# Two seams of a fused forward and backward kernel: the first load of hh's rows issued by GpSimd, backward's tiles cleared in parts by VectorE, dO's tail rows requested earlier

## Chip, cores and metric

The kernel runs on one core of a Trainium2 chip. The metric is the device time of one execution in microseconds; the time before is the median of three runs. Beside the runs there is one execution under the hardware profiler, and every view of the profile that is shown comes from it. TensorE (PE in the views) multiplies matrices, PEld is its loading of weights, VectorE is DVE, ScalarE is ACT, GpSimd is POOL and SyncE is SP. SyncE, ScalarE and GpSimd also issue transfers, each on a queue of its own.

## The reference

The program returns the output of a transformer block and the gradients of its weights and inputs, in bf16 (S = 2048 tokens, D = 512, F = 1792, 32 heads of 128, segments of 32 tokens with 8 memory rows).

```python
mod = (silu(c) @ w_mod).reshape(1, 6, 1, -1)
sa, ca, ga, sb, cb, gb = (mod[:, i] for i in range(6))
h = layernorm(x) * (1 + ca) + sa
x = x + ga * A(h, mem0, Wq, Wk, Wv, Wo)      # attention, segment by segment
h = layernorm(x) * (1 + cb) + sb
x = x + gb * B(h, w_gate, w_up, w_down)

def A(x, mem0, ...):                         # mem goes from segment to segment
    for s in range(S // 32):
        h = concatenate([mem, x[32 * s:32 * s + 32]])
        q, k, v = h @ Wq, h @ Wk, h @ Wv
        o = softmax(mask(q @ k.T * scale)) @ v @ Wo
        mem, out[s] = o[:8], o[8:]

def B(x, w_gate, w_up, w_down):
    hh = sigmoid(x @ w_gate) * (x @ w_up)
    return hh @ w_down

out, vjp = jax.vjp(block, x, mem0, Wq, Wk, Wv, Wo, w_gate, w_up, w_down, c, w_mod)
return out, *vjp(grad_out)
```

## The kernel before, in words

The program is one long stream with several phases. Two places of it matter here.

The first is the end of phase 3, the GLU forward and backward. It is a pipeline over 16 tiles of 128 tokens with seven stages s0 to s6, deepest stage first in each step (`run_pipeline`), so that step `it` runs stage k on tile it - k. Stage s2 makes the rows of hh (tile `hh`), which GpSimd stores to HHROWS in DRAM (L1087); s3 turns hh into `hhT` by a transposing DMA of SyncE (L1098) and makes du and dg (stored by GpSimd to DUROWS and DGROWS); s4 multiplies hhT by w_down (L1120) and turns du and dg into `duT` and `dgT` (L1123, L1124); s5 multiplies those by the turned weights (L1145) and makes dx, which has a single buffer and is stored to DX1ROWS (L1173); s6 sums rows (L1188), turns da (L1192) and stores it as DAOT (L1196, SyncE).

As the pipeline drains, the gradient of w_down begins, 14 chunks of 128 features, each a chain of 16 products over the 16 token tiles (`wd_chunk`, L1216). Its operands are all the rows of hh, loaded back in groups of 384 features (`load_hr`, L1212, 1536 KB in rows of 768 B for group 0), and the rows of db (`dbr`, loaded by ScalarE at L1228). Both lie where w_gate and w_up were (`Wk`). NT is 16: the hook `after(it)` requests dbr after step 17, group 0 after step 18 and group 1 after step 19, and runs a chunk after each of steps 19, 20 and 21. Groups 0 and 1 are SyncE's, the others ScalarE's. The remaining chunks run in the next stage, between transposes of the attention weights (L1380 and L1367, loaded through `stage`, L1376 and L1362), followed by the gradients of w_gate and w_up (L1301).

The second place is the start of phase 4, the backward of attention, 64 turns from the last segment to the first, with the order of every engine's instructions in the loop written by hand (`pin`). Before the loop the tiles are made: dS, dOst, dKT, dQT, Qst and Kst are cleared whole by GpSimd (`ptiles`, L1430), dOT by VectorE (L1435). Each tile has 11 groups of 128 columns (GW), of which 120 are used in most. Then the first rows of dy are projected into `RBds` (L255), turned into `btd` (`turn_b`, L264), spread into dOT (`to_heads`, L65, GpSimd) and copied as tail rows into `dOst` by three small transfers of GpSimd (`dO_tails`, L1546). A last transfer writes zeros from dS to DHA (L1549). A turn's first copies of RAd into dOst are GpSimd's too (L1660); the turn then begins on TensorE with dVT's products (`gv0`, L1616, named g_ps), which read dOst and Pst, then `dp` (L1593), which reads dOT and VT, and so on to dh_ps (L215). `prod` (L1578) on VectorE needs dOT complete. `get_loads` loads OT, Pst and VT of a turn on SyncE (L1514, L1517), `load_rows` Qst and Kst (L1531).

Outside the hand-written orders a scheduler of the tile framework sets each engine's order; in every engine's queue an instruction that waits holds up those behind it.

Of the kernel before, what the change touches and what calls it, by code (L numbers as in the profile page):

```python
# [40 lines left out]
class K:  # L41
# [915 lines left out]
    def phase3(self):  # L957
        nc, tc, cfg, io = self.nc, self.tc, self.cfg, self.io
        D, DC, F, FC, NT, T = cfg.D, cfg.DC, cfg.F, cfg.FC, cfg.NT, cfg.T
# [7 lines left out]
        with ExitStack() as ctx:  # L967
# [8 lines left out]
            i0 = len(self.traced())  # L976
# [7 lines left out]
            def mm():  # L984
                return psM.tile([128, 512], F32, name="mm", tag="m")
# [218 lines left out]
            hrs = {0: hr_0}  # L1204
# [4 lines left out]

            def load_hr(g):  # L1210
                w = min(384, F - 384 * g)
                (nc.sync if g < 2 else nc.scalar).dma_start(hrs[g][:, :, 0:w], self.HHROWS[:, 384 * g:384 * g + w].rearrange("(j p) f -> p j f", p=128))  # L1212

            def wd_chunk(fc, ps, ot):
                for j in range(NT):
                    nc.tensor.matmul(ps[:], lhsT=hrs[fc // 3][:, j, (fc % 3) * 128:(fc % 3) * 128 + 128], rhs=dbr[:, j, :],  # L1216
                                     start=(j == 0), stop=(j == NT - 1))
                self.evac("act" if kk[0] % 2 == 0 else "dve", ot[:], ps[:])
                kk[0] += 1
                nc.gpsimd.dma_start(io["out_9"][fc * 128:(fc + 1) * 128, :], ot[:])  # L1220

            def after(it):
                for f in turns.pop(it, []):
                    f()
                if it == 2:
                    self.pin(i0, [ET.PE, ET.Activation])
                if it == NT + 1:
                    nc.scalar.dma_start(dbr, self.DBROWS[:, :].rearrange("(j p) d -> p j d", p=128))  # L1228
                elif it == NT + 2:
                    load_hr(0)  # L1230
                elif NT + 3 <= it < NT + 6:
                    if it == NT + 3:
                        load_hr(1)
                    wd_chunk(it - NT - 3, mm(), sbp.tile([128, D], BF16, name="ot2", tag="db", bufs=2))
# [5 lines left out]
            def after(it):  # L1240
# [3 lines left out]
                if it >= 5:  # L1244
                    later(it)

            self.run_pipeline(NT, [s0, s1, s2, s3, s4, s5, s6], deepest_first=True, after=after)
            self.pin(i0, [ET.DVE])
            self.pin_behind(i0, self.pinned, [ET.PE, ET.DVE, ET.Activation, ET.Pool, ET.SP])
# [8 lines left out]
        with ExitStack() as ctx:  # L1258
# [6 lines left out]
            def emit_setup():  # L1265
                done[0] += 1
                while setup_pieces and (n_setup - len(setup_pieces)) * n_chunks < done[0] * n_setup:
                    setup_pieces.pop(0)()
            h2r = self.flat(self.Wk, NT * D, NT * D).rearrange("p (j d) -> p j d", j=NT)
            load_hr(2)  # L1270
            xrs = []

# [125 lines left out]
    def phase4(self):  # L1398
        nc, tc, cfg, io = self.nc, self.tc, self.cfg, self.io
        D, DC, H, E, L, M, T, G, NS = cfg.D, cfg.DC, cfg.H, cfg.E, cfg.L, cfg.M, cfg.T, cfg.G, cfg.NS  # L1400
        GW = 128
# [4 lines left out]
        with self.p4_ctx as ctx:  # L1406
# [18 lines left out]
            def ptiles(name, n, zero=True):  # L1425
                ts = []
                for i in range(n):
                    t = pt.tile([128, G * GW], BF16, name=f"{name}{i}")
                    if zero:
                        nc.gpsimd.memset(t[:], 0.0)  # L1430
                    ts.append(t)
                return ts
# [3 lines left out]
            RAd = pt.tile([128, 8 * 128], BF16, name="RAd")  # L1436
            RBds = [pt.tile([128, 8 * 128], BF16, name=f"RBd{i}") for i in range(2)]
            btd = pt.tile([128, 8, 128], BF16, name="btd")
            dSs = ptiles("dS", 1)
            dSTs = ptiles("dST", 1, zero=False)  # L1440
            dOst_t = ptiles("dOst", 1)[0]
            dXTs = {nm: ptiles(nm, n, zero=nm != "dVT") for nm, n in (("dVT", 1), ("dKT", 1), ("dQT", 1))}

            def part3(t, pi):
                return t[:, pi * PW:min((pi + 1) * PW, G * GW)].rearrange("p (g x) -> p g x", x=GW)
# [17 lines left out]
            def to_heads(eng, src, i0, n, r0, w, o):  # L1463

                b = 0 if w == 32 else 96
                s4 = src.rearrange("p i (j r) -> p i j r", r=32)
                d = dOT[:, 120 * i0:120 * (i0 + n)].rearrange("p (i x) -> p i x", x=120)[:, :, b:b + 3 * w]
                self.evac(eng, d.rearrange("p i (j r) -> p i j r", r=w), s4[:, :, 0:3, o:o + w])
                for g in range(3):
                    lo, hi = max(3 * g, i0), min(3 * g + 3, i0 + n, 8)  # L1470
                    if lo < hi:
                        d = dOT[:, 960 + 120 * g + b + w * (lo - 3 * g):960 + 120 * g + b + w * (hi - 3 * g)]
                        self.evac(eng, d.rearrange("p (i r) -> p i r", r=w), s4[:, lo - i0:hi - i0, 3, o:o + w])
# [9 lines left out]
            def proj_b(t, hf, parts=1):  # L1483
                ps = psb.tile([128, 512], F32, name="pass_ps", tag="dh")

                def part(k):
                    self.col_pass(psp, WoT, hf, lambda c: dbs[t][:, c, :, :].rearrange("p s q -> p (s q)"), None, None, ps,
                                  range(k * DC // parts, (k + 1) * DC // parts))

                part(0)  # L1490

                def rest():
                    for k in range(1, parts):
                        part(k)
                    return lambda: self.evac(("act", "dve")[hf], RBds[t % 2][:, 512 * hf:512 * hf + 512], ps[:])

                return rest

            def turn_b(t):
                tps = [self.turn_half(psp, RBds[t % 2], hf) for hf in range(2)]  # L1500

                def f():
                    for hf in range(2):
                        self.evac(("act", "dve")[hf], btd[:, 4 * hf:4 * hf + 4, :], tps[hf][:])
                return f
# [31 lines left out]
            get_loads(NS - 1)  # L1537
            for hf in range(2):
                proj_b(NS // 4 - 1, hf)()()
            turn_b(NS // 4 - 1)()  # L1540
            to_heads("pool", btd[:], 0, 8, 32, 8, 24)

            def dO_tails(s):
                for j in range(3):
                    o = 32 * j + 8 * (s % 4)
                    nc.gpsimd.dma_start(dOst_t[96 + 8 * j:104 + 8 * j, 0:1024], RBds[(s // 4) % 2][o:o + 8, :])  # L1546

            dO_tails(NS - 1)
            nc.gpsimd.dma_start(self.DHA[NS, 0:M, :], dSs[0][0:M, 0:D])  # L1549
            nseg_t = 128 // T  # L1550
            row_stores = []

# [6 lines left out]
            i0 = len(self.traced())  # L1559
            for s in reversed(range(NS)):  # L1560
# [12 lines left out]
                dS, dST, dOst = dSs[0], dSTs[0], dOst_t  # L1573
                dVT, dKT, dQT = dXTs["dVT"][0], dXTs["dKT"][0], dXTs["dQT"][0]
# [160 lines left out]
                g = s // 4  # L1735
# [428 lines left out]
```

## Time and profile before

| what | value |
|---|---|
| runs, median (lowest to highest) | 3083.14 us (3083.08 to 3084.64) |
| profiled execution, its own time | 3080.64 us |
| its span, first to last instruction | 3078.9 us |
| mean granted TensorE clock | 0.991 |
| busy: TensorE, VectorE, GpSimd, ScalarE | 97%, 52%, 45%, 41% of the span |
| DMA | 703.54 MB, mean 229 GB/s |
| end of the GLU pipeline, start of w_down's gradient | about 1300 to 1345 us from the span's start |
| start of the backward turns | about 1524 to 1550 us |
| one later backward turn | 14.90 us (pass_ps at 1549.77 and 1564.67) |

A line of a view gives the engine, the line of the kernel, the operation, and `out<-in` by the names of tiles. In a list in order of time the first two numbers are start and duration in us; what stands in brackets is the idle time before it and what ended that. SPq, ACTq and POOLq are the engines' queues in which transfers are issued; a transfer's duration there is that of its issue, and its data land later. The list of waits has the waiting line, what released it, the total, the number of times and the longest. The windows give for each stretch the busy time of every engine with the number of instructions, the granted clock (1.00 is full speed), the busy share of the DMA engines, which can pass 1 in a short window, and GB/s.

### The profile page before, as it was taken

Reading aid. Unit: us, or ns where it says so; the run is one execution under the profiler, and the core shown is the slowest. Engines: PE = TensorE matmul, PEld = TensorE weight load, DVE = VectorE, ACT = ScalarE, POOL = GpSimd, SP = SyncE. Lnnn points to the kernel's source line nnn. Section 1 sums busy time; section 2 is a strip of 40 time slices with the busy share of each in tenths; the row PEclk is TensorE's granted clock in tenths of the full one; section 3 lists DMA queues with packets and bytes.
Section 4 is the critical chain, followed back from the end, with each engine's and each line's share of the span. In section 5 each row is a group of like instructions: output and inputs, shape, how many; then the busy total and the mean of one; then the engine's idle time right before and its main releaser. Section 6 shows DMA issues by size and latency. Waiting matters only on the chain.

```text
span 3078.9 us, 106050 instructions
## 1 busy us (share of the span) xinstructions
PE 2985.9 (97%) x43769; PEld 1821.5 (59%) x43845; DVE 1613.0 (52%) x3799; ACT 1254.4 (41%) x3056; POOL 1386.1 (45%) x2960
## 2 busy tenths in 40 slices
PE   6999999999999799989899999999999999999999
PEld 3666666666665444445577777777777754445455
DVE  4556656665655788742255555555555632322221
ACT  2555555555555433322155555555555520111011
POOL 3666767667766222211244444444444422333322
PEclk8999999999999899999999999999999999999999
DMA  8888788788778799997599999999999998666574
GB/s 300 217 215 204 204 209 217 203 214 212 206 202 255 199 229 231 225 282 254 176 232 246 244 247 246 245 248 244 248 243 245 253 278 278 201 194 221 188 236 149
DMA packets 845992, 703.54 MB, mean 229 GB/s; under 512 B 544354, under 2 KB 717954, under 8 KB 845124
## 3 DMA queue, kind: packets, MB, share of 16 engines
q1 hardware_dynamic: 714196, 486.69, 62.7%
q0 software_dynamic: 60656, 148.64, 15.1%
q10 hardware_dynamic: 70656, 61.41, 6.4%
q8 instruction: 345, 5.65, 0.8%
q14 instruction: 139, 1.14, 0.1%
HBM read 294.93 MB, written 276.35 MB: 186 GB/s over the span
## 4 chain that ended last, share of the span: by engine, by line
PE 45%; issue 3%; POOL 1%; DMA 1%; DVE 0%; ACT 0%; SPq 0%; POOLq 0%
PE gps L1954 9%; PE dh_ps L215 8%; PE g_ps L1616 6%; PE pass_ps L255 5%; PE gps5o L1968 5%; PE dhq_ps L223 4%; PE dh_tps L215 3%; PE dp_ps L1593 2%; PE tps L1526 2%; PE dp_ps L1601 1%; PE turn_ps L1480 1%; PE dh_ft L323 1%; POOL out_dram L1958 1%; DMA dhb<-DHA 0%; PE turn_ps L264 0%
## 5 line engine op out<-in xcount | busy, mean ns | idle before, releaser
L1954 PE MATMUL gps<-rows,hrows 128*128 128x512 bf16 (+2 forms) x2124 | 415.6, 355 | 1.9
L1954 PEld LDWEIGHTS <-hrows 128*128 128x128 bf16 x2160 | 211.3, 98 | 204.5
L255 PEld LDWEIGHTS <-hT 128*32 128x32 bf16 x6144 | 158.3, 97 | 168.5 <-DMA Wq<-in_A_Wq_dram 5.5
L1660 POOL COPY dOst<-RAd 96x512 bf16<-96x512 bf16 x128 | 75.5, 613 | 311.4 <-DVE RAd L63 311.2
L63 DVE CAST ot<-gps 128x512 bf16<-128x512 f32 (+3 forms) x76 | 48.1, 633 | 286.9 <-PE gps L1954 188.4
L1958 POOL DMA_DIRECT2D out_dram<-ot x108 | 81.5, 755 | 255.9 <-DVE ot L63 137.2
L61 ACT ACTIVATE ot<-gps 128x512 bf16<-128x512 f32 (+3 forms) x75 | 41.3, 551 | 352.3 <-PE gps L1954 230.7
L909 POOL TENSOR_TENSOR Pst<-Pst,rden 120x1408 bf16<-120x1408 bf16 x63 | 159.7, 2536 | 47.7 <-issue 21.4
L61 ACT ACTIVATE dVT<-g_ps 128x480 bf16<-128x480 f32 (+1 forms) x192 | 104.7, 545 | 95.5 <-PE g_ps L1616 95.1
L63 DVE CAST RA0v<-pass_ps 128x512 bf16<-128x512 f32 x128 | 88.5, 692 | 91.2 <-PE pass_ps L255 85.3
L255 PE MATMUL pass_ps<-Wv,hT 128*32 128x512 bf16 x2048 | 134.2, 382 | 0.0
L215 PE MATMUL dh_ps<-WvT,dVT 128*32 128x512 bf16 x2048 | 133.4, 380 | 0.3 <-DVE RBd L63 0.2
L255 PE MATMUL pass_ps<-Wq,hT 128*32 128x512 bf16 x2048 | 123.3, 383 | 5.3 <-DMA Wq<-in_A_Wq_dram 5.3
L1968 PE MATMUL gps5o<-WoT,rows 128*128 128x512 bf16 x580 | 127.7, 379 | 0.6
L223 PE MATMUL at_ps<-Wo,OT 128*32 128x256 bf16 x4096 | 124.6, 274 | 3.0 <-DMA Wo<-in_A_Wo_dram 3.0
L255 PE MATMUL pass_ps<-Wk,hT 128*32 128x512 bf16 x2048 | 121.6, 379 | 2.2 <-ACT hT L899 1.1
L255 PE MATMUL pass_ps<-WoT,dyT 128*32 128x256 bf16 (+1 forms) x3072 | 122.4, 308 | 0.9 <-ACT dyT L1734 0.9
L223 PE MATMUL dhq_ps<-WqT,dQT 128*32 128x256 bf16 x4096 | 122.9, 273 | 0.0
L215 PE MATMUL dh_ps<-WkT,dKT 128*32 128x512 bf16 x2048 | 122.3, 380 | 0.0
L223 PEld LDWEIGHTS <-dQT 128*32 128x32 bf16 x4096 | 109.6, 97 | 15.9
L1603 DVE SCALAR_TENSOR_TENSOR dS<-dp_ps,Pst_l 128x480 bf16<-128x480 f32 (+1 forms) x192 | 106.1, 608 | 19.2 <-PE dp_ps L1601 19.2
L223 PEld LDWEIGHTS <-OT 128*32 128x32 bf16 x4096 | 103.8, 97 | 18.6 <-issue 6.5
(421 smaller groups left out, 7034.9 us busy)
## 6 DMA issues: line engine op xcount, KB each, us to landing
OSR<-Ost SPq DMA_DIRECT2D x64, 352.0 KB
OT<-OT SPq DMA_DIRECT2D x64, 352.0 KB
VT<-VTr SPq DMA_DIRECT2D x64, 352.0 KB
PS<-Pst SPq DMA_DIRECT2D x64, 352.0 KB
OT_l<-OT SPq DMA_DIRECT2D x64, 352.0 KB
Pst_l<-PS SPq DMA_DIRECT2D x64, 352.0 KB
VT_l<-VT SPq DMA_DIRECT2D x64, 352.0 KB
DVR<-rows_x POOLq DMA_DIRECT2D x64, 352.0 KB, 6.2
```

Of the source, the lines that this page charges most:

```text
L61: return nc.scalar.activation(out, in_, AF.Copy)
L63: return nc.vector.tensor_copy(out, in_)
L215: self.nc.tensor.matmul(ps[32 * j:32 * j + 32, :], lhsT=lhsT, rhs=w, start=(n < 4), stop=(n >= total - 4), tile_position=(0, 32 * j))
L223: nc.tensor.matmul(ps[32 * j:32 * j + 32, :], lhsT=x[k], rhs=w[k][:, 256 * d:256 * d + 256], start=(n == 0), stop=(n == total - 1), tile_p ...
L255: self.nc.tensor.matmul(ps[32 * j:32 * j + 32, :], lhsT=lhs(c), rhs=rhs, start=(c == 0), stop=(c == DC - 1), tile_position=(0, 32 * j))
L909: nc.gpsimd.tensor_tensor(Pst[0:120, :, :], Pst[0:120, :, :], rden[:, :].unsqueeze(2).to_broadcast([120, G, 128]), op=ALU.mult)
L1603: nc.vector.scalar_tensor_tensor(out=part3(dS, pi)[:, :, 0:120], in0=ps[:, 0:n, 0:120], scalar=cfg.scale, in1=part3(Pst, pi)[:, :, 0:120], ...
L1616: nc.tensor.matmul(ps[:, j, 0:w], lhsT=lh[:, g * GW:(g + 1) * GW], rhs=rh[:, g * GW:g * GW + w], start=True, stop=True)
L1660: nc.gpsimd.tensor_copy(dOst[0:96, 512 * hf:512 * hf + 512], RAd[0:96, 512 * hf:512 * hf + 512])
L1954: nc.tensor.matmul(ps[:, 0:ng * E], lhsT=hrows[:, tp_, c * 128:(c + 1) * 128], rhs=rows[:, tp_, 0:ng * E], start=(tp_ == 0), stop=(tp_ == ...
L1958: nc.gpsimd.dma_start(outw[c * 128:(c + 1) * 128, h0:h0 + 3 * (ng - 1) + 1:3, :], ot[:, 0:ng * E].rearrange("p (h e) -> p h e", e=E))
L1968: nc.tensor.matmul(pss[gg][:], lhsT=src[0][:, src[1], gg * E:(gg + 1) * E], rhs=dyrows[:, tp_, :], start=(tp_ == order[0]), stop=(tp_ == o ...
```

## The change

In the GLU's drain, group 0 of hh's rows is requested by GpSimd in place of SyncE, and after step 17 in place of step 18, right behind the request of dbr. Group 1 stays with SyncE, the others with ScalarE.

At the start of backward, none of dS, dOst, dKT and dQT is cleared by GpSimd. VectorE clears dOst whole, of dS the 32 rows by 512 columns that DHA's zeros are read from, and in dS, dKT and dQT the last 8 of every 128 columns. Qst and Kst stay with GpSimd. The three transfers of dO's tail rows now come before the turn of RBds and its spreading into dOT, and GpSimd's order there is pinned.

```diff
             def load_hr(g):
                 w = min(384, F - 384 * g)
-                (nc.sync if g < 2 else nc.scalar).dma_start(hrs[g][:, :, 0:w], self.HHROWS[:, 384 * g:384 * g + w].rearrange("(j p) f -> p j f", p=128))
+                (nc.gpsimd, nc.sync, nc.scalar)[min(g, 2)].dma_start(hrs[g][:, :, 0:w], self.HHROWS[:, 384 * g:384 * g + w].rearrange("(j p) f -> p j f", p=128))
...
                 if it == NT + 1:
                     nc.scalar.dma_start(dbr, self.DBROWS[:, :].rearrange("(j p) d -> p j d", p=128))
-                elif it == NT + 2:
                     load_hr(0)
                 elif NT + 3 <= it < NT + 6:
...
-            dSs = ptiles("dS", 1)
+            dSs = ptiles("dS", 1, zero=False)
             dSTs = ptiles("dST", 1, zero=False)
-            dOst_t = ptiles("dOst", 1)[0]
-            dXTs = {nm: ptiles(nm, n, zero=nm != "dVT") for nm, n in (("dVT", 1), ("dKT", 1), ("dQT", 1))}
+            dOst_t = ptiles("dOst", 1, zero=False)[0]
+            nc.vector.memset(dOst_t[:], 0.0)
+            dXTs = {nm: ptiles(nm, n, zero=False) for nm, n in (("dVT", 1), ("dKT", 1), ("dQT", 1))}
+            nc.vector.memset(dSs[0][0:32, 0:D], 0.0)
+            for t in (dSs[0], dXTs["dKT"][0], dXTs["dQT"][0]):
+                nc.vector.memset(t[:].rearrange("p (g x) -> p g x", x=GW)[:, :, 120:GW], 0.0)
...
             for hf in range(2):
                 proj_b(NS // 4 - 1, hf)()()
-            turn_b(NS // 4 - 1)()
-            to_heads("pool", btd[:], 0, 8, 32, 8, 24)
 
             def dO_tails(s):
                 for j in range(3):
                     o = 32 * j + 8 * (s % 4)
                     nc.gpsimd.dma_start(dOst_t[96 + 8 * j:104 + 8 * j, 0:1024], RBds[(s // 4) % 2][o:o + 8, :])
 
+            i0 = len(self.traced())
             dO_tails(NS - 1)
+            turn_b(NS // 4 - 1)()
+            to_heads("pool", btd[:], 0, 8, 32, 8, 24)
             nc.gpsimd.dma_start(self.DHA[NS, 0:M, :], dSs[0][0:M, 0:D])
+            self.pin(i0, [mybir.EngineType.Pool])
```

## The prediction

> **What bounds the kernel now.** I read the page's head first, then the list of TensorE's waits, then the order of time around the two places that the diff touches, then the busy time and clock in short windows there. The head:
>
> ```profile
> span 3078.9 us, 106050 instructions
> PE 2985.9 (97%) x43769; PEld 1821.5 (59%) x43845; DVE 1613.0 (52%) x3799; ACT 1254.4 (41%) x3056; POOL 1386.1 (45%) x2960
> ```
>
> TensorE is busy 97% of the span, so an edit that leaves its products alone can win only its idle time and the time in which it runs slowly. Two of its longest waits (line: us in total, times, longest) lie in the two places:
>
> ```profile
> PE g_ps L1616 <- DMA dOst<-RBd: 6.6, 1, 6.6
> ...
> PE mm L1216 <- DMA Wk<-HHROWS: 4.1, 1, 4.1
> ```
>
> Seam 1 is the start of w_down's gradient. SyncE's queue in order of time (start, duration of the issue):
>
> ```profile
> 1306.73 3.32 SPq L1124 DMA_TRANSPOSE dgT<-dg  x1
> 1310.15 0.54 SPq L1196 DMA_DIRECT2D DAOT<-daT  x1
> 1310.85 2.39 SPq L1098 DMA_TRANSPOSE hhT<-hh  x1
> 1313.42 1.06 SPq L1212 DMA_DIRECT2D Wk<-HHROWS  x1
> 1315.14 3.27 SPq L1196 DMA_DIRECT2D DAOT<-daT  x1
> 1318.53 6.98 SPq L1123 DMA_TRANSPOSE duT<-du  x1
> ```
>
> The load of hh's rows is requested at 1313.42 and TensorE starts on it at 1325.49: 12.07 us. The rows' last store was issued by GpSimd at 1300.92, which then had nothing until 1310.99:
>
> ```profile
> 1300.92 0.54 POOL L1087 DMA_DIRECT2D HHROWS<-hh  x1 [3.02 <-DVE hh L1086]
> 1310.99 0.54 POOL L1173 DMA_DIRECT2D DX1ROWS<-dx  x1 [9.54 <-DVE dx L1172]
> ```
>
> Seam 2 is backward's first turn. GpSimd clears six tiles, copies heads, and only then requests dO's tail rows:
>
> ```profile
> 1524.37 1.27 POOL L1430 MEMSET dS<- 128x1408 bf16 x1 [0.32 <-PE wtp L1367]
> ...
> 1531.65 1.17 POOL L65 COPY dOT<-btd 128x192 bf16<-128x192 bf16 x4
> 1532.76 1.54 POOL L1546 DMA_DIRECT2D dOst<-RBd  x3
> 1534.30 0.50 POOL L1549 DMA_DIRECT2D DHA<-dS  x1
> 1534.79 1.17 POOL L1660 COPY dOst<-RAd 96x512 bf16<-96x512 bf16 x2
> ```
>
> The chain of waits has the third request at 1533.79, 3.03 us of transfer, 0.20 us, and the product at 1537.03; TensorE had stopped at 1530.36. After both stops it runs slowly (windows: length, busy of PE, PEld, DVE, ACT, POOL, then clock, DMA share, GB/s):
>
> ```profile
> 1326.00:1327.00 1.00, 0.78 (x3) 0.35 (x3) 0.00 (x0) 0.00 (x0) 0.31 (x1) 0.50 1.78 301
> 1533.00:1534.00 1.00, 0.00 (x0) 0.00 (x0) 0.20 (x1) 0.00 (x0) 1.00 (x3) 0.62 0.86 220
> 1538.00:1539.00 1.00, 1.00 (x13) 1.00 (x12) 0.00 (x0) 0.20 (x1) 0.35 (x1) 0.50 0.07 16
> ```
>
> The clock halves 2.9 us after the last product in seam 2 (0.62 as the mean of 1533 to 1534 puts it at 1533.24), some 3.6 us after it in seam 1, and is back about 3 us after work resumes. In seam 1 the first chunk's 16 products took 1325.49 to 1330.49, 5.00 us; at full clock the next 23 took 5.13 with the last one's 0.38 in it, 0.216 from start to start, so 16 take 3.45: 1.55 lost. In seam 2 the first turn took 3.26 us from its first product (1537.03) to dh_ps (1540.29), the second turn 1.88 (1553.31 to 1555.19): 1.38 lost. At stake: 4.10 + 1.55 + 6.67 + 1.38 = 13.7 us, 0.44%.
>
> **Seam 1, the load.** Removed: one issue of 1.06 us from SyncE. Added: one on GpSimd, ahead of DX1ROWS, DUROWS and DAROWS. Its 2048 rows of 768 B cost GpSimd between 1.09 us (w_down's load, 1792 rows) and 1.6 (out_dram's 0.755 for some 490 rows against 0.542 for 128, drawn out): I take 1.2, hidden in the 9.54 us before DX1ROWS. Ahead of it GpSimd waits until the last store of hh has landed: 4.6 us by that line's landing row, 6.0 by DX1ROWS's, so 1305.5 to 1306.9. Nothing is queued behind the wait until 1310.99. The load then needs 12.07 us by its own row; the loads that GpSimd issued of w_gate and w_up, 1792 KB each, took 10.2 and 12.6. It lands at 1317.6 to 1319.5, before TensorE's 1321.39. The stores behind it in GpSimd's queue land later; dx has one buffer, and DX1ROWS must leave it before 1322.13, which 2.6 us allow. SyncE gains: DAOT's 3.27 and duT's 6.98 stood behind this load in one queue, and duT was not needed until 1331.05 (1325.4 now).
>
> What is late next is hhT, wanted at 1318.21. Its issue ended at 1313.24; now dgT and hhT share the engines with the load. With another queue's load beside them transposes took 2.39 to 3.94. At 3.94 each hhT's issue ends at 1315.5, and with 3.0 of landing (dO's row) it is there at 1318.5: 0.3 late; I take 0.5. Ends: 0 (slack holds), and 6.98 each, as behind the load: issue end 1321.6, there at 1324.6, 6.4 late with 1.5 of half clock.
>
> Then the transfers give something back. DMA's share is 0.91 to 1.15 in every 5 us from 1300 to 1335, so the same bytes cannot end much sooner; it idles 2.65 us in 1336 to 1340, ahead of the Wo loads that TensorE's progress releases. TensorE 5.15 sooner uses that idle and leaves 2.5 of backlog; windows of 1342 to 1354 hold 1.4 of idle to absorb it, and the remaining 1.1 lengthens the 3.9 us wait on stage at 1362.75. Ends: 0 and 2.5. Sum of seam 1: -4.10 - 1.55 + 0.5 + 1.1 = -4.05. Its ends are -5.65 and, with the late hhT, +2.2 (chunk over at 1324.6 + 3.2 + 1.5 + 3.45 = 1332.7 for 1330.49).
>
> The Trainium skill ("DMA: Bandwidth & Descriptors", section "Issuing engines are not separate DMA queues") says that the three issuers share 16 engines and another issuer saves only issuing time; taken alone it makes seam 1 nothing and the time 3077.0. Against it stands that the request itself waited until 1313.42. Its page "SBUF — State Buffer", section "SBUF: two separate sides", says that VectorE's two-port operations keep GpSimd from writing descriptors; HHROWS's issue took its usual 0.542 while VectorE ran umh (1300.65 to 1301.74), so I add nothing, where the rule could add up to 2.8 us (VectorE's stretch from 1306.35 to 1309.16) and make the load land at 1320.4 to 1322.3.
>
> **Seam 2, clearing and order.** Four of GpSimd's clearings go (1.22 us apart): the last ends at 1526.86. VectorE gets five behind dOT's (664 words, 0.61): dOst 704 words 0.65, dS 256 words 0.27, three of 44 words 0.09 each by the line through that row and dyT's (16 words, 0.07): 1.2 us. They fit into its idle 1525.57 to 1526.64, bar 0.1, so RBd ends at 1527.45; without that cover all 1.2 would delay RBd and the tail rows. The tail requests follow at 1527.5, three of 0.51, the third at 1528.53. The heads (1.17) move behind them, 1529.1 to 1530.2, DHA to 1530.7, the copies of RAd to 1531.9; none is late. prod, which waits for the heads, runs from 1530.3.
>
> Moved on SyncE, as the built order shows: Qst's and Kst's loads now stand before VT_l, which slips from 1525.21 to 1527.3, behind Kst's clearing. The five loads up to it are 1716 KB, about what the windows from 1525 to 1531 moved (1.85 MB), so it ends near 1530.7; dp needs it from 1532.7. No cost, some 2 us of slack for the landing.
>
> The tail rows then travel beside those loads: 3.03 us by the seam's own row (share 0.8), 4.8 as the loop's median (share 1.0, but behind DQR's store in the same queue), 6.2 as its worst. I take 3.6: product at 1528.53 + 3.6 + 0.2 = 1532.3. TensorE idles 1.9 us, less than the 2.9 after which the clock fell, so I take it to stay. Sum: -4.73 - 1.38 = -6.1. Ends: -6.7 (3.03) and -2.1 (6.2: 1534.9, half clock again). The loop's 63 later turns keep their order and waits.
>
> **Sum.** -4.05 - 6.1 = -10.15. The profiled execution took 3080.64 (span 3078.9), so it would take 3070.5; the runs' median is 3083.14, 2.5 above it, and gives 3073.0.
>
> **Rivals.**
> R1, hhT takes the load's place: +2.2 - 6.1, 3079.2. For it: duT's 6.98; against: that was one shared queue, and GpSimd's is another.
> R2, the tail rows are slow among the loads: -4.05 - 2.1, 3077.0. For it: DMA share 1.0 in 1530 to 1532; against: nothing stands before them in their queue.
> R3, seam 1 is bound by bytes and gives all back: -6.1, 3077.0. For it: the full share; against: the idle 2.65.
> R4, slower: the load starves in GpSimd's queue behind the turns of two others. That queue moved 6.60 MB in 1270 to 1350, 82 GB/s; at half of it 1.57 MB take 38.4 us, landing at 1344.4 for 1325.5: +18.9 - 6.1, 3095.9. It decides from a landing after 1331.6 (no gain) and 1337.8 (0.2% slower). Against: 10.2 and 12.6 for w_gate and w_up.
>
> **Numbers.** 0.2% (6.2 us) is about what a measurement tells from no change, so faster means under 3077.0. Forecast 0.55 (3069.5 to 3076.5 alone), R1 0.13, R2 0.13, R3 0.09, R4 0.10. R2 and R3 sit on the border and are halved: faster 0.55 + 0.11 = 0.66; same 0.24; slower 0.10. The range 3069.0 to 3081.0 leaves out R4 and the tails of R1 and the forecast.
>
> **What would show it.** Right: L1216's wait on Wk under 1 us with clock 1.00 there, GpSimd's load issued at 1305 to 1307, the wait on dOst<-RBd near 2 us with clock 1.00 in 1532 to 1540. Wrong: a new wait at L1120 on hhT, the stage wait grown beyond 5 us, VectorE's clearings ending after 1526.9, or dp waiting on VT_l. A change in the pitch of the backward turns (14.90 us) would break the whole sum: 0.1 us there is 6.3 us.

## The result, and the profile after

| | before | changed |
|---|---|---|
| runs, median (lowest to highest), us | 3083.35 (3081.64 to 3090.30), 13 runs | 3088.69 (3084.39 to 3098.55), 13 runs |
| ratio, 95% interval | | 1.0018 (1.0011 to 1.0025) |
| profiled execution, its span, us | 3080.64, 3078.9 | 3090.49, 3088.7 |

The change costs some 5.5 us, where I had forecast a gain of 10. The head of the page says that no engine's work has grown much:

```profile
PE 2989.4 (97%) x43845; PEld 1821.6 (59%) x43845; DVE 1614.3 (52%) x3804; ACT 1253.4 (41%) x3056; POOL 1379.5 (45%) x2957
```

TensorE's waits say where the time went (line, what released it, total in us, times, longest). The 4.1 us of L1216 on the rows of hh are gone; in their place stands a wait nearly three times as long, and the wait on dO's tail rows is 1.7 us shorter than before, not 4.7:

```profile
PE mm L1120 <- DMA hhT<-hh: 11.5, 1, 11.5
...
PE g_ps L1621 <- DMA dOst<-RBd: 4.9, 1, 4.9
```

At seam 1, in order of time, SyncE's queue, then GpSimd's, then the products:

```profile
1303.64 3.65 SPq L1124 DMA_TRANSPOSE dgT<-dg  x1
1307.38 0.54 SPq L1196 DMA_DIRECT2D DAOT<-daT  x1
1308.08 9.71 SPq L1098 DMA_TRANSPOSE hhT<-hh  x1
1317.85 0.57 SPq L1196 DMA_DIRECT2D DAOT<-daT  x1
1318.52 9.40 SPq L1123 DMA_TRANSPOSE duT<-du  x1
```

```profile
1298.04 0.54 POOL L1087 DMA_DIRECT2D HHROWS<-hh  x1 [3.02 <-DVE hh L1086]
1305.91 1.19 POOL L1212 DMA_DIRECT2D Wk<-HHROWS  x1 [7.34 <-PE mm L1120]
1308.11 0.55 POOL L1173 DMA_DIRECT2D DX1ROWS<-dx  x1 [1.01 <-DVE dx L1172]
...
1311.37 0.54 POOL L1110 DMA_DIRECT2D DUROWS<-du  x1
...
1313.77 0.54 POOL L1111 DMA_DIRECT2D DGROWS<-dg  x1 [0.46 <-DVE dg L1109]
```

```profile
1328.25 4.60 PE L1120 MATMUL mm<-Wv,hhT 128*128 128x512 bf16 x14 [11.47 <-DMA hhT<-hh]
1332.68 3.62 PE L1216 MATMUL mm<-Wk 128*128 128x512 bf16 x16
```

The load goes out on time and is no longer waited for. hhT's issue takes 9.71 us instead of 2.39, and its data are there 20.2 us after the issue began (1308.08 to 1328.25). Two windows of the DMA engines (packets, MB, mean rate, packets below a size; then each queue's packets, MB, share of 16 engines; q0 is GpSimd's, q1 SyncE's, q10 ScalarE's, and a transpose moves in packets of 256 B, 1792 of them for hhT; the store of DAOT, which stands between dgT and hhT in SyncE's queue, sends 512 of the same size) show two different troubles. The first is 1309 to 1312:

```profile
DMA packets 238, 0.94 MB, mean 313 GB/s; under 512 B 35, under 2 KB 35, under 8 KB 238
## 3 DMA queue, kind: packets, MB, share of 16 engines
q0 software_dynamic: 203, 0.94, 97.6%
q1 hardware_dynamic: 35, 0.00, 1.0%
```

The load has the engines whole, and SyncE's queue, in which DAOT and hhT come next, moves next to nothing (of the 35 small packets 26 are of 4 B). The second is 1315 to 1320, when the load is over and GpSimd's stores, held up behind it, run beside hhT:

```profile
DMA packets 509, 0.35 MB, mean 71 GB/s; under 512 B 463, under 2 KB 464, under 8 KB 509
```

71 GB/s in place of some 300: now both crawl. Packet by packet (own tabulation of the trace), 256 B packets took 58 to 145 ns on average in three of these five microseconds, and the stores' 4096 B packets 416 to 1148 ns in four of them; undisturbed they take 18 and 160. Counted in the order of the queue (DAOT's 512 packets, then hhT's 1792), hhT's own packets began to move at 1314.5, when the load had 0.8 us to go, and took 11.4 us; in the kernel before they took 3.3.

At seam 2 the chain of waits has the third tail request at 1540.49:

```profile
1540.49 6.09 DMA dOst<-RBd
1546.58 0.25 issue
1546.82 0.56 PE g_ps L1621 x4
```

3.03 us of transfer have become 6.09, and the clock halved again (0.57 as the mean of 1546 to 1550).

### The profile page after: what moved, and what is told of

It reads as the page before. It is cut to its first block, busy times and chain, and to the rows that moved or that the text cites. A ratio compares the mean times of both kernels' runs of the same rounds, so it can differ in the third digit from the quotient of the medians.

```text
span 3088.7 us, 106123 instructions
## 1 busy us (share of the span) xinstructions
PE 2989.4 (97%) x43845; PEld 1821.6 (59%) x43845; DVE 1614.3 (52%) x3804; ACT 1253.4 (41%) x3056; POOL 1379.5 (45%) x2957
## 3 DMA queue, kind: packets, MB, share of 16 engines
q0 software_dynamic: 61024, 150.22, 15.2%
q8 instruction: 345, 5.65, 0.8%
## 4 chain that ended last, share of the span: by engine, by line
PE 90%; DMA 5%; DVE 3%; issue 1%; ACT 1%; POOL 0%; SPq 0%; DVEq 0%; POOLq 0%; ACTq 0%
PE pass_ps L255 18%; PE gps L1959 13%; PE dh_ps L215 8%; PE g_ps L1621 6%; PE gps5o L1973 4%; PE at_ps L223 4%; PE dhq_ps L223 4%; PE gps L1300 3%; PE mm L1145 3%; PE dh_tps L215 3%; PE turn_ps L264 2%; PE dp_ps L1598 2%; PE tps L1529 2%; PE mm L1120 2%; PE tps L742 2%; PE mm L1105 1%
```

## The experiments

All kernels were measured in one way: the time against before (ratio with its 95% interval), and from each one's profile the lengths of four stretches, in us. A: from the issue of HHROWS's last store to the first product behind chunk 0. B: from there to backward's first clearing, a stage that no kernel's edits but seam 1's can reach. C: from that clearing to the first dh_ps. D: from that clearing to the third turn's first product, so that it contains C. "hhT" is the wait of L1120 on hhT.

| kernel | ratio (95%) | A | hhT | B | C | D |
|---|---|---|---|---|---|---|
| before | 1 | 30.1 | none | 193.3 | 15.9 | 43.8 |
| changed | 1.0018 (1.0011 to 1.0025) | 38.8 | 11.5 | 198.8 | 14.4 | 42.2 |
| e1 load only | 1.0026 (1.0016 to 1.0036) | 38.2 | 11.3 | 193.6 | 16.5 | 44.4 |
| e2 start only | 0.9998 (0.9990 to 1.0007) | 32.2 | none | 193.0 | 14.4 | 42.2 |
| e3 rows apart | 1.0025 (1.0015 to 1.0036) | 39.2 | 11.8 | 192.0 | 15.6 | 43.5 |
| e0 no load | 0.9979 (0.9970 to 0.9988) | 24.8 | none | 192.7 | 16.5 | 45.0 |
| e4 ScalarE, 768 B rows | 1.0002 (0.9993 to 1.0011) | 31.4 | 4.2 | 192.4 | 17.2 | 45.5 |
| e5 ScalarE, 3584 B rows | 0.9993 (0.9984 to 1.0002) | 30.3 | 3.4 | 193.2 | 15.9 | 44.7 |
| e9 load behind stores | 1.0012 (1.0003 to 1.0021) | 35.1 | none | 196.7 | 15.9 | 44.4 |
| e10 stores by ScalarE | 1.0001 (0.9992 to 1.0010) | 31.7 | 3.5 | 196.2 | 16.0 | 44.8 |
| e7 second loads later | 1.0027 (1.0015 to 1.0038) | 38.4 | 11.0 | 193.1 | 11.7 | 42.6 |
| e8 second loads by GpSimd | 0.9989 (0.9981 to 0.9998) | 32.2 | none | 192.4 | 10.8 | 38.6 |
| e11 load split | 0.9987 (0.9978 to 0.9996) | 24.4 | none | 196.3 | 15.9 | 44.8 |
| e12 both | 0.9968 (0.9956 to 0.9980) | 24.4 | none | 194.9 | 12.6 | 40.4 |

Kernels with the same code at a place differ there by up to 2 us in A (before, e2 and e8) and by up to 7 in B, so a single profile is read to no better than that.

**Which half costs (e1, e2).** e1 is before with the change's edit of `load_hr` alone, e2 is before with the change at backward's start alone.

> The change to the rows of hh alone; backward's start as before. If the loss sits here, as the two traces read: hhT's issue takes 9 to 10 us instead of 2.4, the products on hhT wait 11 to 12 us for it, and the kernel is 6 to 9 us slower than before (0.2 to 0.3%). If the load is not to blame and the profiled run of the changed kernel was a stray one: hhT's issue 2.4 to 4 us, 3 to 5 us faster than before.

> The change to backward's start alone; the rows of hh as before. As the two traces read, first clearing to the first sum of dh takes 14.4 us instead of 15.9: 1.5 us faster than before, which with the noise of a run is 0 to 3 us. As I predicted it, 6 us faster, with the products on dOst waiting 1.9 us; the trace of the changed kernel has 4.9.

The load alone is 0.26% slower (8 us), A is 8 us longer and hhT's issue takes 8.91 us. The start alone is 0.02% faster, with an interval from 3.1 us gained to 2.2 lost; its products wait 4.72 us on the tail rows. So the whole loss is seam 1's. B's 5.4 us in the profile of the changed kernel are not the change's: e1 and e7 have the same code there and 193.6 and 193.1.

**Is it the packets' size (e3, e5)?** My first theory was that 256 B packets starve beside large ones, because the load's own packets were 4608 B. e3 sets the buffer's rows apart:

```diff
-            hr_0 = self.flat(self.Wk, NT * D, NT * 384).rearrange("p (j f) -> p j f", j=NT)
+            hr_0 = self.flat(self.Wk, NT * D, NT * CH).rearrange("p (j f) -> p j f", j=NT)
```

> As the load alone, but the buffer's rows of 384 stand 448 apart, so that a packet can't run over several of them: the same bytes, by the same queue, at the same moment, in packets of 768 B. Theory 1 (the transposes' 256 B packets starve beside 4 KB packets): hhT's issue 3 to 5 us, the products on hhT wait under 4 us, time within 3 us of before or up to 4 us under it. Theory 2 (any load laid beside the transposes takes their bytes' place): hhT's issue 8 to 10 us and 9 to 12 us of wait, 6 to 9 us slower than before, as with the large packets.

hhT waited 11.8 us, but the test did not bite: the packets stayed 4608 B (GpSimd's queue has 61024 in the page, as in the changed kernel). It settles nothing about size. e4 and e5 do. Both request the load by ScalarE, whose rows travel as they are, one packet each, and pin SyncE's order behind it:

```diff
-                (nc.sync if g < 2 else nc.scalar).dma_start(hrs[g][:, :, 0:w], ...
+                (nc.scalar, nc.sync, nc.scalar)[min(g, 2)].dma_start(hrs[g][:, :, 0:w], ...
```

and for e5, in place of `load_hr(0)`:

```diff
+                    nc.scalar.dma_start(self.flat(self.Wk, NT * D, 3 * F).rearrange("p (j f) -> p j f", j=3), self.HHROWS[13 * 128:, :].rearrange("(j p) f -> p j f", p=128))
```

> The load requested early by ScalarE (about 1 us behind where GpSimd requests it in the change), in its own queue: 768 B packets, and GpSimd's stores not behind it. Theory 1 (256 B packets starve beside 4 KB packets): hhT's issue 3 to 5 us, its products wait under 5 us. Theory 2 (any early load takes the transposes' bytes): hhT's issue 7 to 10 us, wait 8 to 12 us, 5 us or more slower than before. Theory 3 (GpSimd's queue: the load goes ahead of the transposes whole, and the stores held up behind it then run beside them, where both crawl): as theory 1, hhT's issue 3 to 5 us, the stores landing within 7 us.

> As the early load by ScalarE, but of 3 blocks of whole rows, 3584 B each (1.38 MB; chunks 0 to 2 are other numbers). Theory 1: hhT's issue 7 to 10 us and 8 to 12 us of wait, as in the change. Theory 2: the same, 7 to 10 us. Theory 3: 3 to 5 us, as with the small rows.

Packets of 768 B or 3584 B: waits of 4.2 and 3.4 us, issues of 6.12 and 6.05 (no theory had named an issue between 5 and 7). The size of the load's packets is out; e10 below adds 4608 B, from GpSimd, with 3.5 us. But all are well above before: part of theory 2 holds. The DMA engines of e4 in 1311 to 1313:

```profile
DMA packets 859, 0.66 MB, mean 330 GB/s; under 512 B 0, under 2 KB 859, under 8 KB 859
...
q10 hardware_dynamic: 859, 0.66, 107.2%
```

Not one packet of SyncE's queue moves in these two microseconds, though the load is in another queue and has 768 B packets. That is the first of the two troubles, worth some 4 us of wait whoever requests the load. It does not last to the load's end: counted as above, DAOT's packets moved beside the load's last third, and hhT's began 0.4 us before its last packet. From 1314 to 1320 the rest of the load, GpSimd's stores and SyncE's packets share the engines well, and hhT's packets took 4.8 us:

```profile
DMA packets 3044, 2.16 MB, mean 360 GB/s; under 512 B 2317, under 2 KB 2821, under 8 KB 3044
...
q1 hardware_dynamic: 2237, 0.57, 42.0%
q10 hardware_dynamic: 520, 0.39, 19.1%
```

(In these two the scheduler also set da's transposes and sums among hhT's products and b_bf ahead of tb, so I read them by hhT and not by the total.)

**What makes 4 us into 11 (e10, e9).** In e10 GpSimd's early load stays and the five stores behind it go to ScalarE's queue:

```diff
-                nc.gpsimd.dma_start(self.DUROWS[r0:r1, :], du[:])
-                nc.gpsimd.dma_start(self.DGROWS[r0:r1, :], dg[:])
+                (nc.scalar if j == NT - 1 else nc.gpsimd).dma_start(self.DUROWS[r0:r1, :], du[:])
+                (nc.scalar if j == NT - 1 else nc.gpsimd).dma_start(self.DGROWS[r0:r1, :], dg[:])
```

and likewise o_sb's for j == NT - 2, dx1's and da's for j == NT - 3. In e9 the load stays GpSimd's too, but after step 18 and pinned behind those stores:

```diff
-                    load_hr(0)
+                    load_hr(0); self.pin(self.i_p, [ET.Pool])
```

> GpSimd's early load as in the change, with the five stores that stood behind it in GpSimd's queue (of dx1, da, du, o_sb and dg, 1.4 MB) requested by ScalarE in its own. If the stores held up behind the load and then running beside hhT make the difference between 11.5 us of wait and ScalarE's 4 (theory 3): hhT's issue 6 to 7 us, its products wait 2 to 6 us, time within 3 us of before. If GpSimd's load by itself slows transposes more than ScalarE's does: still 9 us or more of issue and 10 to 12 us of wait, 6 to 9 us slower than before.

> GpSimd's load, but requested behind its five stores (the last is dg's) instead of ahead of them: some 8 us later than in the change, 3 us later than SP in before. If the queue's order is what hurts (theory 3): hhT is there before its products as in before, its issue 2.2 to 2.5 us, no wait on it; chunk 0 waits 4 to 9 us for the load, and the time is 0 to 5 us over before. If a load by GpSimd's queue slows transposes wherever it stands: duT or dgT take its place, and the kernel is 6 us or more slower than before.

In e10 the wait is that of ScalarE's early load, and the time is that of before:

```profile
PE mm L1120 <- DMA hhT<-hh: 3.5, 1, 3.5
```

TensorE's, VectorE's and GpSimd's other instructions stand in the order of e1. My number for the issue was wrong (9.06 us, not 6 to 7): an issue can be long while the data are there 11.8 us after its start. In 1315 to 1320 its engines moved 1.35 MB where the changed kernel's moved 0.35:

```profile
DMA packets 3291, 1.35 MB, mean 269 GB/s; under 512 B 2930, under 2 KB 3188, under 8 KB 3291
...
q1 hardware_dynamic: 2874, 0.72, 87.8%
```

(dg's store, 0.46 of the 1.4 MB, left ScalarE only at 1318.38, behind daT; so it was out of hhT's way for another reason.) In e9, with the stores ahead, nothing waits on hhT, whose issue takes 2.54 us; now chunk 0 waits 5.6 us for the load and dgT's issue takes 10.13 us beside it. So it is not GpSimd's queue as such, but what stands behind the load in it: some 4 of the 11 us are the load going first, and the other 7 come with the five stores queued behind it.

That much of theory 3 is shown. Its mechanism, stores that slow hhT by moving beside it, is not. While hhT's packets moved (counted as above), 1.18 MB of GpSimd's stores moved beside them in e4 as in the changed kernel, yet hhT took 4.8 us in the one and 11.4 in the other. In e10, where it took 2.7, the stores went in smaller packets (1024 to 3584 B, where GpSimd's are of 4096 and 7168 B) and only 0.13 MB of them met it. And SyncE's queue was slow with no other queue beside it, in e10 in 1323 to 1325, where dgT is due:

```profile
DMA packets 631, 0.16 MB, mean 80 GB/s; under 512 B 631, under 2 KB 631, under 8 KB 631
...
q1 hardware_dynamic: 631, 0.16, 123.7%
```

**What there was to win (e0, e11).** e0 leaves out the load (`hrs = {0: dbr[:, :, 0:384]}`, and no `load_hr(0)`).

> Before without the first load of hh's rows: chunks 0 to 2 of the GLU weight gradients take columns of dbr, already on the chip, in its place (so 384 rows of that output are other numbers). It shows what this load costs at most. If the 4.1 us wait and the half clock behind it are all that the load does: 4 to 6 us faster than before, hhT's issue 2.2 to 2.5 us as before. If chunk 0 then waits for dbr or the transposes instead: 0 to 2 us.

It is 0.21% faster (6.5 us), and A is 5.3 us shorter. The gain that I priced at 5.65 was there. e11 goes for it in another way: chunk 0 needs only 128 of the 384 columns.

```diff
-                    load_hr(0)
+                    load_hr(0); self.i_sp = len(self.traced())
...
-                        load_hr(1)
+                        load_hr(0, 128, hr_1); load_hr(1)
```

Here `load_hr(0)` takes the 128 columns only, `hr_1` holds the other 256, and SyncE's order from there on is pinned as written.

> Before, with the load split: the 128 columns that chunk 0 needs (0.5 MB) where SP requested all 384, the other 256 behind dgT, the last transposes. If a load only has to be small and behind the transposes that are due first: chunk 0 waits under 1 us instead of 4.1 to 4.7, 3 to 6 us faster than before. If the stores and duT beside it keep the engines (as without the load, where they crawled at 104 to 140 GB/s): 2 to 4 us of wait are left, 0 to 2 us faster.

```profile
1315.30 3.18 PE L1120 MATMUL mm<-Wv,hhT 128*128 128x512 bf16 x14
1318.32 3.62 PE L1216 MATMUL mm<-Wk 128*128 128x512 bf16 x16
...
1322.43 3.19 PE L1145 MATMUL mm<-Wq,duT 128*128 128x512 bf16 x14
```

No wait between hhT's products and chunk 0, none behind it, full clock; A is as short as without the load. Chunk 1 then waits 2.7 us for the other columns, and B is 3 us above before's, within its spread. 0.13% faster (0.04 to 0.22).

**Seam 2 (e7, e8).** What is late there are the tail rows' transfers, and beside them travel the second turn's three loads, 1.08 MB that nobody needs yet. e7 is the whole change with these loads behind Qst's next one; e8 is e2 with them issued by GpSimd behind its copies of RAd.

```diff
-                if s > 0:
+                if 0 < s < NS - 1:
                     get_loads(s - 1)
...
-                load_rows(Qst_t, self.QST, s - 1)
+                load_rows(Qst_t, self.QST, s - 1); s == NS - 1 and get_loads(s - 1)
```

```diff
-                    nc.gpsimd.tensor_copy(dOst[0:96, 512 * hf:512 * hf + 512], RAd[0:96, 512 * hf:512 * hf + 512])
+                    nc.gpsimd.tensor_copy(dOst[0:96, 512 * hf:512 * hf + 512], RAd[0:96, 512 * hf:512 * hf + 512]); s == NS - 1 and hf and get_loads(s - 1, nc.gpsimd)
```

> The whole change, with the second turn's three loads (1.08 MB) requested behind Qst's next load, 14 us later. If dO's tail rows are late because they stand among these loads' packets: the products on dOst wait 1 to 2.5 us instead of 4.9, and the kernel is 2 to 4 us faster than the change as it is. If 6 us is what such a gather takes by itself: still 4 to 5 us of wait, and the time of the change.

> The new start of backward alone, with the second turn's three loads requested by GpSimd behind its copies of dO (some 4 us later than SP did) instead of behind Qst's next load, where the 1.8 us won were given back in the two turns that followed. Expected: the products on dOst wait 2.5 to 3.5 us instead of 4.7, first clearing to first sum of dh 12 to 13 us, later turns 14.9 us as before; 3 to 5 us faster than before. If the loads are late again: the second turn over 16.5 us, no gain.

e7's wait falls to 3.10 us, not to the 1 to 2.5 that I expected, and C from 14.4 to 11.7. But D stays at 42.6: the second set now comes so late that the next two turns pay the gain back, and the time is that of the change. e8 keeps it. Its chain of waits has 3.83 us of transfer, and the product starts after 2.57 us of wait at full clock:

```profile
1533.56 0.37 PE L1622 MATMUL g_ps<-Pst_l,dOst 128*128 128x120 bf16 x4 [2.57 <-DMA dOst<-RBd]
```

C is 5.1 us under before and D 5.2 (38.6 for 43.8), so nothing is given back: 0.11% faster (0.02 to 0.19).

**Both (e12).** e11's split load and e8's start in one kernel.

> The split load together with the new start of backward and the second turn's loads by GpSimd behind dO's copies. If the two seams add up: 6 to 11 us faster than before (0.2 to 0.36%). If either is given back in the stage between: 2 to 4 us.

0.32% faster than before (0.20 to 0.44): 3073.32 us, median of 6 runs, for 3083.64. It beats both kernels. Its start of backward is not as good as e8's alone (C 12.6 for 10.8): the third request took 4.16 us, TensorE waited 2.9, and its clock fell to 0.50. Why is not shown.

## Why the prediction was wrong

**Seam 1, the load itself: right, but for its start.** GpSimd's wait and issue were as priced (issue 1.19 us for 1.2), with hh's last store landing 7.3 us after its issue, where I had 4.6 to 6.0. That the load still went out within my 1305 to 1307 was luck: the store itself came 2.9 us earlier in this run (1298.04 for 1300.92). The load's last packet moved at 1315.3, 9.4 us after its issue began, where I had 12.07. R4, the load starving in that queue, did not come.

**Seam 1, hhT: the step that failed.** "With another queue's load beside them transposes took 2.39 to 3.94." Those are durations of issues, and I read them as transfers. From them I took hhT to be 0.5 us late, 6.4 at worst; it was waited for 11.5 us, a sign of being wrong that the prediction had named first. In the trace of before duT's issue runs from 1302.63 beside dbr's load; its engines in 1301 to 1306:

```profile
DMA packets 1424, 1.51 MB, mean 303 GB/s; under 512 B 0, under 2 KB 1415, under 8 KB 1424
```

No packet of a transpose, while dbr moved; duT's first came at 1306.8, 4.2 us after its issue began and with 1.8 us of dbr's load to go. And in 1308 to 1312, when dbr was all but over:

```profile
DMA packets 4037, 1.05 MB, mean 261 GB/s; under 512 B 3993, under 2 KB 4037, under 8 KB 4037
```

So the trace of before already showed that a transpose's data can stand for most of the load beside it. dbr's load cost nothing: TensorE did not wait for duT or dgT. hhT had 2.6 us to spare (its last packet at 1315.6, wanted at 1318.21): a load of 1.57 MB at the rate of those windows takes some 5 us, and ScalarE's load cost 3.4 to 4.2 of wait.

**Seam 1, the stores: named but not priced.** "The stores behind it in GpSimd's queue land later" was in the prediction, checked against dx's buffer only. With them behind the load 4 us became 11 (e1 against e10). My worst end for hhT, 6.4 us late, was drawn from transposes behind a load in one queue and left this out; A grew by 8.1 to 9.0 in four kernels (38.2 to 39.2 for 30.1), against +2.2 at that end.

**Seam 1, the giving back (1.1 us at the stage) and R3.** The changed kernel could not show either, since TensorE came later at the stage and not sooner. Where it came sooner, B is 0.6 us under before's in e0 and 3.0 and 1.6 above it in e11 and e12, all within B's spread, so the 1.1 stays undecided. Against R3 speaks e11, which moves the same bytes and is 4.0 us faster in the whole. R1, hhT taking the load's place, was right in kind and far too cheap.

**Seam 2: right in its steps, one term mis-sized.** VectorE's clearings took 0.65 + 0.27 + 3 x 0.10 = 1.22 us for 1.2, VT_l made no wait, and from the third turn to the end it took 1510.9 us for 1510.7. The term was the tail rows' transfer: taken 3.6, measured 6.09; the wait was 4.87 for 1.9, and the clock fell, which I had taken to stay. That is R2's end (6.2). The requests were also 0.8 us later than planned, 4.94 us behind the first clearing for 4.16. Measured gain: 1.5 to 1.6 us for 6.1. With the second set of loads out of the way (e8) it is 5.2.

The Trainium skill ("DMA: Bandwidth & Descriptors", section "Queues, rings and completion order") says that each DMA engine takes turns between the queues that have work, one packet at a time. I had leaned on no such rule, but it would have made SyncE's queue and the load share the engines from the start. These runs show otherwise for most of the load (0 packets under 512 B in 2 us in e4, 35 in 3 us in the changed kernel), and the measurement decides; in the load's last third e4's two queues did share.

What stays open: why SyncE's queue stands for most of a load beside it, and what the crawl is. The crawl is not the load's: without the load (e0) duT, dgT and the stores moved 145 GB/s in 1318 to 1325. Nor does it come with every meeting of stores and transposes, as e4 shows (360 GB/s), nor only with one, as e10 shows (80 GB/s). What tells these apart was not tried.

## What to carry to other kernels

The duration of a transfer's issue says little of when its data move: count its packets in short windows (by their size, and with an eye on other transfers of the same size) before calling a transfer cheap beside another. A load requested earlier can go ahead of what is needed sooner, in another queue too, and holds up what stands behind it in its own; ask of both who needs them first. It paid more to load less (128 columns for the first chunk, the rest behind the last transposes) and to hold back loads that nobody needs yet than to ask sooner for everything.

## What the hardware showed that I had not expected

- A 128 x 1792 transpose by DMA (1792 packets of 256 B) moved nothing, or next to it, during most of a load of 1.4 to 2.1 MB in another queue, be its packets 768, 1024, 3584 or 4608 B. With little beside it SyncE's queue moved some 1000 such packets per us (3993 under 512 B in 4 us).
- GpSimd's queue moved the load's rows of 768 B in packets of 4608 B, six times as large, also into a buffer whose rows stood apart; the queues of SyncE and ScalarE sent each row as a packet.
- Transposes and stores together moved 71 GB/s in one 5 us stretch, 145 over 7 us in another kernel, and 360 in a third, there with the end of a load among them.
- The same third request of tail rows, 16 KB, took 3.03, 3.83 or 6.09 us, by what else had been requested around it.
